# A reordered attention loop: fewer TensorE mode switches per head pair, q/k turned two pairs ahead, both heads normalised at once, V staging buffers of their own

## The chip, the cores and the metric

The kernel runs on one core of a Trainium2 chip. The metric is device time in microseconds (us) of one execution; a profile adds the "span", from the first to the last instruction, which is about 1.7 us shorter than the time. A single core has no second, slower die to be compared with, so the state of a run is judged by its time: one that is more than 1.5% above the fastest run of the same kernel is marked slow. Each kernel has one profile, of its first run (that of before is of a run apart); three that I use fell in runs marked slow (before, and the experiments e3 and f1).

## The reference, cut to what matters

Causal attention with 16 extra "beacon" keys and values in front, for 8 batches of 8 heads (576 tokens, 64 wide), then a soft mixture of experts over the 4608 tokens of width 512: 8 experts with 4 slots each.

```python
k_all = concat([beacon_k, k]); v_all = concat([beacon_v, v])
a = softmax(q @ k_all.T / 8, causal over the 576 own keys)
x = (a @ v_all) as 4608 x 512
logits = x @ phi                                # 4608 x 32
d = softmax(logits, over tokens);  slot_input = d.T @ x
for e in range(8):
    slot_out[e] = relu(slot_input[e] @ w1[e]) @ w2[e]
out = softmax(logits, over slots) @ slot_out
```

## The kernel before

The loop works on 32 pairs of heads. For one pair it makes scores in four "score steps" (K x Q products into PSUM, then an exp on ACT; step 0 also gets a causal mask on POOL), multiplies by V with a column of ones ("attend", which gives the sums too), divides by the sums on DVE, and turns the result ("xt_piece") for the logits. q and k of a later pair are transposed on TensorE in a 64-row mode ("transp"); the score steps are 64-row work too, nearly everything else is 128-row work (dt is 32-row). Once per batch of four pairs there are three more pieces: logits, the turned weights d ("dt"), and the sums for the slots ("si"). All of the expert weights are read during the loop into one large tile, the arena. Then come the expert stage and the output stage.

`vbuf[1]`, the landing place of V for odd batches, is a piece of the arena, and so are the q/k slots:

```python
arena = const.tile([P, E * 8192], F16, name="arena")
# load_pair: q and k of pair n go to arena[:, o:o + ...]         (five slots)
vmore = const.tile([P, TK * D], F16, name="vmore")
vbuf = [vmore[:, :], arena[:, vend:vend + TK * D]]
...
def load_bv(b):                       # beacon V: every fourth partition
    nc.gpsimd.dma_start(out=vbuf[b % 2][0:4 * H:4, 0:Nb * D], in_=beacon_v[b]...)
```

The order of one pair (cut):

```python
score(n, 0);  xt_piece(n - 2);  score(n, 1)
transp(n + 1)
attend(n - 1, 0)                      # reciprocal and product of head 0
score(n, 2)
attend(n - 1, 1)                      # reciprocal and product of head 1
score(n, 3)
load_pair(n + 5)
```

`avs` are two tiles of one PSUM bank each, `scs` two tiles of two banks each:

```python
avs = [ps_av.tile([P, 512], FP, name=f"av{i}") for i in range(2)]
scs = [ps_sc.tile([P, 2, 512], FP, name=f"sc{i}") for i in range(2)]
...
sop = avs[0]                                        # sum of the second layers
def first_layer(e):
    hp = avs[1] if e % 2 else scs[0][:, 0, :]       # hidden layer of expert e
    ...16 matmuls into hp, then Relu on ACT: hp -> hbuf
for e in range(E + 2):
    first_layer(e)       # if e < E
    turn_hidden(e - 1)   # 2 transposes, 1 copy
    second_layer(e - 2)  # 8 matmuls into sop
```

The softmax here doesn't subtract the row's maximum and nothing guards it: scores larger than these inputs give would overflow.

## Time and profile before

| | before |
|---|---|
| time of the runs, us | 227.32 median (225.67 to 228.94) |
| span of the profile, us | 231.3 (this run, of 233.0 us, is marked slow) |
| first mask of pair 0 to that of pair 5 | 35.1 |
| first mask of pair 5 to that of pair 31 | 132.0 |
| slot sums ready to expert outputs ready ("expert stage") | 16.5 |

The first mask of a pair is a good milestone, because POOL does exactly one such mask per pair, after the first exp. It is not exact: when POOL is held by its DMA issues, the mask comes later than the exp's end (in before by 1.1 to 3.3 us in pairs 0, 1, 2, 8 and 24).

The page's head, busy time per engine and the slices of the TensorE clock and of DMA (one digit is 1/40 of the span, 9 is 90% or more):

```profile
span 231.3 us, 7829 instructions
...
PE 169.4 (73%) x3400; PEld 119.7 (52%) x3400; DVE 145.8 (63%) x365; ACT 135.4 (59%) x187; POOL 88.6 (38%) x151
...
PEclk9999999999979999956999999799999967999965
DMA  6999299998599999969899994998699990029996
```

No engine is full. The DMA row dips to 2, 5, 6 and 4 in slices 5, 11, 18 and 25 (of 5.8 us each), in a stretch where there is always something left to load: something holds loads back there.

The list of waits (engine, line, what it waited for: us in total, times, longest), first TensorE's, its weight loads (PEld) and its matmuls (PE):

```profile
PEld L240 <- DMA arena<-in_beacon_v_dram: 9.6, 4, 3.2
PE tr L240 <- DMA arena<-in_beacon_v_dram: 8.3, 4, 3.0
```

And the waits of the queue on SP that issues q and k loads:

```profile
SPq L90 <- DMA arena<-in_beacon_v_dram: 40.5, 4, 10.5
```

Line 240 is the q/k transposes, line 90 the q/k loads. Neither has any business with beacon V. The timeline around the second of the four occurrences (start, duration, engine, line, operation, in brackets the idle time before and what ended it):

```profile
61.70 0.53 POOL L143 DMA_DIRECT2D arena<-in_beacon_v_dram  x1 [3.45 <-DMA arena<-in_k_dram]
...
63.55 0.78 PE L240 MATMUL tr<-idb,arena 64*64 64x64 bf16 x36 [3.00 <-DMA arena<-in_beacon_v_dram]
63.56 0.33 SPq L90 DMA_DIRECT2D arena<-in_q_dram  x1
```

POOL sits 3.45 us until all k loads in flight have landed, then issues one small load; TensorE and the q/k queue are released together when it has landed. It is a fence in both directions, and it occurs four times, once per odd batch. Even batches use the same strided load into another tile and have no such wait.

Stretches of the windows view (length, busy time of each engine with its number of instructions, granted clock, DMA share, GB/s landed):

```profile
core 0: us, PE busy (x) PEld busy (x) DVE busy (x) ACT busy (x) POOL busy (x), PEclk, DMA share, GB/s
58.00:64.00 6.00, 2.56 (x66) 1.79 (x66) 2.99 (x8) 3.26 (x4) 2.54 (x5) 1.00 0.49 86
64.00:100.00 36.00, 31.40 (x713) 23.63 (x708) 28.43 (x70) 24.74 (x36) 19.33 (x33) 0.93 1.05 263
188.00:204.40 16.40, 13.66 (x244) 7.01 (x245) 3.66 (x11) 10.33 (x8) 0.00 (x0) 0.82 0.16 33
...
196.00:200.00 4.00, 3.72 (x91) 2.41 (x92) 1.09 (x5) 2.54 (x3) 0.00 (x0) 1.00 0.01 4
```

Inside a fence the DMA share is 0.49; outside it is about 1. The third row is the expert stage: 16.4 us and clock 0.82. It starts at 0.50 and, as the last row shows, is at 1.00 in its second half.

Away from fences a pair takes about 4.6 us. TensorE has no long wait there, but each score step and each transposition waits a little for DVE or ACT:

```profile
131.50 0.40 PE L255 MATMUL sc<-qT,kT 64*128 64x128 bf16 x8 [0.24 <-ACT ex L261]
132.12 0.43 PE L304 MATMUL tr<-idh,xb 128*128 128x128 f16 x5 [0.22 <-DVE xb L290]
```

### The profile page before, as it was taken

The numbers are of one execution on the slowest core, as the hardware profiler recorded it, in microseconds if no ns is written. First come the engines' busy times: TensorE is split into PE (matmuls) and PEld (weight loads), VectorE is DVE, ScalarE is ACT, GpSimd is POOL, SyncE is SP. The second block draws the span as 40 slices with busy tenths as digits, with TensorE's granted clock in tenths as the row PEclk, the third lists the DMA queues.
The fourth block names the chain that finished last, engine by engine and source line by source line (L and its number), as shares of the span: only waits on it lengthen the run. The fifth ranks groups of instructions, "written<-read, shape, count | busy, mean of one in ns | idle before, by whom it ended". The sixth has DMA issues, their size and how long they took to land.

```text
span 231.3 us, 7829 instructions
## 1 busy us (share of the span) xinstructions
PE 169.4 (73%) x3400; PEld 119.7 (52%) x3400; DVE 145.8 (63%) x365; ACT 135.4 (59%) x187; POOL 88.6 (38%) x151
## 2 busy tenths in 40 slices
PE   2624469888498998799988986988898759878300
PEld 1413257666285766577666664756766535433100
DVE  4409267868566997875689777568966622279500
ACT  2531416796548678744966877395797338659400
POOL 8380435454448545433647435253464300000000
PEclk9999999999979999956999999799999967999965
DMA  6999299998599999969899994998699990029996
GB/s 203 247 312 243 27 240 263 207 258 203 91 225 280 244 283 288 257 131 207 246 205 262 265 270 114 201 316 152 106 198 213 214 192 7 3 99 422 415 424 272
DMA packets 20049, 50.89 MB, mean 220 GB/s; under 512 B 5169, under 2 KB 5169, under 8 KB 18992
## 3 DMA queue, kind: packets, MB, share of 16 engines
q0 software_dynamic: 7776, 21.77, 50.0%
q1 hardware_dynamic: 12096, 28.35, 34.0%
q8 instruction: 26, 0.43, 0.7%
q10 hardware_dynamic: 144, 0.29, 0.3%
q14 instruction: 7, 0.06, 0.1%
HBM read 62.71 MB, written 9.44 MB: 312 GB/s over the span
## 4 chain that ended last, share of the span: by engine, by line
PE 32%; DMA 26%; DVE 22%; ACT 8%; issue 3%; SPq 1%; POOL 1%; DVEq 0%; POOLq 0%; ACTq 0%
PE av L282 9%; DMA arena<-in_k_dram 7%; PE tr L240 6%; DMA phif<-in_moe_phi_dram 6%; PE sc L255 6%; DVE xb L290 5%; DVE arena L515 4%; DMA arena<-in_q_dram 4%; ACT ex L261 4%; DMA arena<-in_beacon_v_dram 3%; DMA vmore<-in_v_dram 3%; DVE qT L242 3%; DVE vh L133 3%; PE tr L304 3%; DVE kT L242 3%
## 5 line engine op out<-in xcount | busy, mean ns | idle before, releaser
L261 ACT ACTIVATE ex<-sc 128x1024 f16<-128x1024 f32 (+3 forms) x128 | 106.0, 868 | 66.5 <-PE sc L255 66.3
L263 POOL TENSOR_SCALAR_AFFINE_SELECT ex<-ex 128x1024 f16<-128x1024 f16 x32 | 35.1, 1095 | 65.7 <-ACT ex L261 65.7
L255 PE MATMUL sc<-qT,kT 64*128 64x128 bf16 (+5 forms) x576 | 48.9, 267 | 6.8 <-ACT ex L261 5.4
L282 PEld LDWEIGHTS <-ex 128*128 128x128 f16 (+2 forms) x960 | 40.8, 114 | 11.2 <-issue 10.0
L282 PE MATMUL av<-vh,ex 128*128 128x65 f16 (+1 forms) x896 | 45.0, 207 | 2.1 <-DVE vh L133 2.1
L240 PE MATMUL tr<-idb,arena 64*64 64x64 bf16 x1152 | 29.7, 204 | 20.8 <-DMA arena<-in_beacon_v_dram 8.3
L242 DVE COPY qT<-tr 128x576 bf16<-128x576 bf16 x32 | 24.2, 757 | 27.4 <-PE tr L240 27.4
L240 PEld LDWEIGHTS <-arena 64*64 64x64 bf16 x1152 | 25.4, 118 | 28.9 <-issue 11.7
L290 DVE TENSOR_TENSOR xb<-av,r 128x320 f16<-128x320 f32 x64 | 31.5, 492 | 2.2
L255 PEld LDWEIGHTS <-kT 64*128 64x128 bf16 (+1 forms) x576 | 21.2, 105 | 18.3 <-issue 11.9
L242 DVE COPY kT<-tr 128x576 bf16<-128x576 bf16 x32 | 24.0, 750 | 1.7 <-PE tr L240 1.5
L308 DVE COPY xT<-tr 128x592 f16<-128x592 f16 x32 | 14.4, 449 | 8.6 <-PE tr L304 8.6
L304 PE MATMUL tr<-idh,xb 128*128 128x128 f16 (+1 forms) x160 | 14.7, 226 | 4.6 <-DVE xb L290 4.4
L161 POOL DMA_DIRECT2D arena<-in_moe_w_dram x32 | 17.8, 556 | 0.0
L289 DVE RECIPROCAL r<-av 128x5 f32<-128x5 f32 x64 | 12.1, 190 | 5.2 <-PE av L282 4.7
L304 PEld LDWEIGHTS <-xb 128*128 128x128 f16 (+1 forms) x160 | 9.6, 101 | 9.8 <-DVE xb L290 8.5
L282 PE MATMUL av<-vt,ex 80*80 80x65 f16 x64 | 13.6, 213 | 0.9 <-DVE vt L133 0.9
L133 DVE STREAM_TRANSPOSE vh<-vmore 128x512 f32<-128x512 f32 x8 | 8.8, 1122 | 7.2 <-DMA arena<-in_v_dram 7.2
L513 ACT ACTIVATE arena<-fp,rc 128x512 f32<-128x512 f32 x18 | 11.3, 686 | 3.4 <-PE fp L511 2.7
L515 DVE TENSOR_SCALAR arena<-fp,rc 128x512 f32<-128x512 f32 x18 | 12.3, 746 | 0.7 <-PE fp L511 0.7
L511 PE MATMUL fp<-soh,eLh 128*128 128x512 f16 x36 | 10.6, 377 | 2.4 <-ACT arena L513 1.5
L269 POOL TENSOR_SCALAR_AFFINE_SELECT ex<-ex 80x160 f16<-80x160 f16 x32 | 10.3, 323 | 2.6 <-ACT ex L261 2.3
(66 smaller groups left out, 143.0 us busy)
## 6 DMA issues: line engine op xcount, KB each, us to landing
arena<-in_moe_w_dram POOLq DMA_DIRECT2D x32, 512.0 KB, 8.7
arena<-in_q_dram SPq DMA_DIRECT2D x32, 288.0 KB, 7.1
arena<-in_k_dram SPq DMA_DIRECT2D x31, 288.0 KB, 8.7
out_dram<-arena SPq DMA_DIRECT2D x8, 1024.0 KB, 8.6
arena<-in_v_dram POOLq DMA_DIRECT2D x20, 128.0 KB, 6.5
vmore<-in_v_dram POOLq DMA_DIRECT2D x15, 128.0 KB, 6.8
out_dram<-arena SPq DMA_DIRECT2D x2, 512.0 KB, 3.0
arena<-in_k_dram ACTq DMA_DIRECT2D x1, 288.0 KB, 2.7
```

Of the source, the lines that this page charges most:

```text
L133: nc.vector.transpose(out=dst[:, e], in_=src.bitcast(FP).rearrange("p (j e) -> p e j", j=TK)[:, e])
L161: nc.gpsimd.dma_start(out=arena[:, wloc[m]:wloc[m] + WP], in_=src)
L240: nc.tensor.transpose(tp[po:po + 64, j, :], hi, idb[po:po + 64, po:po + 64])
L242: nc.vector.tensor_copy(out=dst[:, Nb:Nb + S].rearrange("p (s j) -> p s j", j=J), in_=tp[:, :, :].rearrange("p j s -> p s j"))
L255: nc.tensor.matmul(sc[0:kn, a, col:col + un], kT[n % 3][64 * a:64 * a + 64, P * c:P * c + kn], qT[n % 3][64 * a:64 * a + 64, u0:u0 + un], ...
L261: nc.scalar.activation(ex[n][:, :, o:o + w], sc[:, :, 0:w], AF.Exp, scale=scale)
L263: nc.gpsimd.affine_select(out=ex[n][:, :, 0:512].rearrange("p a (c t) -> p a c t", c=4), in_=ex[n][:, :, 0:512].rearrange("p a (c t) -> p ...
L282: nc.tensor.matmul(avs[a][0:m, i * DD:(i + 1) * DD], ex[n][0:kn, a, o:o + m], vchunk(b, h, c, kn), start=(c == 0), stop=(c == i))
L290: nc.vector.tensor_tensor(out=xb[b % 2][:, :, h, :], in0=avv[:, :, 0:D], in1=r5[:, :].unsqueeze(2).broadcast_to([P, NCH, D]), op=AL.mult)
L304: nc.tensor.transpose(tp[:, i, 0:m], xb[b % 2][0:m, i, 2 * g:2 * g + 2, :].rearrange("p h d -> p (h d)"), idh[0:m, 0:m])
L308: nc.vector.tensor_copy(out=xT[b][:, g, :], in_=tp[:, :, :].rearrange("p i u -> p (i u)")[:, 0:U])
L515: nc.vector.tensor_scalar(out=osb[:, j, :], in0=fp_[:, :], scalar1=rc[:, i:i + 1], scalar2=None, op0=AL.mult)
```

## The change

The intent: switch TensorE between 64-row and 128-row work twice per pair instead of six times, by putting score steps 3, 0 and 1 and the q/k transposes next to each other; turn q and k two pairs ahead instead of one; normalise both heads with one reciprocal and one product; give both V buffers tiles of their own; land the first V batch so that beacons need no strided load. The diff, cut to its core:

```diff
-    vmore = const.tile([P, TK * D], F16, name="vmore")
-    vbuf = [vmore[:, :], arena[:, vend:vend + TK * D]]
-    vlast = arena[:, vend + TK * D:vend + 2 * TK * D]
+    vbuf = [const.tile([P, TK * D], F16, name=f"vbuf{i}") for i in range(2)]
+    vlast = arena[:, vend:vend + TK * D]
+    vto = vend + TK * D
...
-    vt = [const.tile([P, 4 * H, DP], F16, name=f"vt{i}") for i in range(2)]
+    vt = [arena[:, vto:vto + 4 * H * DP].rearrange("p (r d) -> p r d", d=DP),
+          const.tile([P, 4 * H, DP], F16, name="vt1")]
...   # first V batch: partitions in order (chunk, head); its beacons in partitions 0..7
-    wloc = [...] + [lend + WP * x for x in (3, 4, 5, 6, 7, 0, 1, 2)]
+    wloc = [...] + [lend + WP * x for x in (6, 7, 3, 4, 5, 0, 1, 2)]
...
-    avs = [ps_av.tile([P, 512], FP, name=f"av{i}") for i in range(2)]
+    av = ps_av.tile([P, 2, 512], FP, name="av")
...   # transp: beacon columns of kT copied by POOL first, not by DVE last
...   # attend: both heads, then
+        r5 = sml.tile([P, 2, NCH], FP, name="r5", tag="r5")
+        nc.vector.reciprocal(out=r5[:, :, :], in_=avv[:, :, :, D])
+        nc.vector.tensor_tensor(out=xb[b % 2][:, :, 2 * g:2 * g + 2, :]..., in0=avv[:, :, :, 0:D], ...)
...   # the loop
+        score(n, 0)
+        score(n, 1)
+        xt_piece(n - 2)
+        attend(n - 1)
+        score(n, 2)
+        transp(n + 2)
+        load_pair(n + 7)
+        score(n, 3)
+        # then, once per batch each: logits (two halves), dt_piece, si_piece
...   # the expert stage
-    sop = avs[0]
+    sop = av[:, 0, :]
-        hp = avs[1] if e % 2 else scs[0][:, 0, :]
+        hp = av[:, 1, :] if e % 2 else scs[0][:, 0, :]
```

More of the change, by code (lines that the diff above doesn't have):

```diff
@@ L106, in load_v @@
     def load_v(b, qd):
-        main = vbuf[b % 2]
-        lo = (32 * qd - Nb) * D
-        if b == 0 and qd == 0:
-            nc.gpsimd.dma_start(out=main[0:1, Nb * D:TK * D], in_=vrows[0:1, 0:(TK - Nb) * D])
+        lo = b * H * S * D + (32 * qd - Nb) * D
+        hs_, cs_ = [S * D, H], [4 * TK * D, 4]
+        if b > 0:
             nc.gpsimd.dma_start(
-                out=main[1:4, :],
-                in_=bass.AP(tensor=v.tensor, offset=v.offset + lo + 4 * TK * D,
-                            ap=[[4 * TK * D, 3], [1, TK * D]]))
-            nc.gpsimd.dma_start(
-                out=main[4:32, :],
-                in_=bass.AP(tensor=v.tensor, offset=v.offset + S * D + lo,
-                            ap=[[S * D, H - 1], [4 * TK * D, 4], [1, TK * D]]))
-            return
@@ L120, in load_v @@
-        nc.gpsimd.dma_start(
-            out=main[32 * qd:32 * qd + 32, :],
-            in_=bass.AP(tensor=v.tensor, offset=v.offset + b * H * S * D + lo,
-                        ap=[[S * D, H], [4 * TK * D, 4], [1, TK * D]]))
+                out=vbuf[b % 2][32 * qd:32 * qd + 32, :],
+                in_=bass.AP(tensor=v.tensor, offset=v.offset + lo, ap=[hs_, cs_, [1, TK * D]]))
+        elif qd > 0:
+            nc.gpsimd.dma_start(
+                out=vbuf[0][32 * qd:32 * qd + 32, :],
+                in_=bass.AP(tensor=v.tensor, offset=v.offset + lo, ap=[cs_, hs_, [1, TK * D]]))
+        else:
+            nc.gpsimd.dma_start(out=vbuf[0][0:H, 0:Nb * D],
+                                in_=beacon_v[0].rearrange("h n d -> h (n d)"))
+            nc.gpsimd.dma_start(out=vbuf[0][0:H, Nb * D:TK * D], in_=vrows[0:H, 0:(TK - Nb) * D])
+            nc.gpsimd.dma_start(
+                out=vbuf[0][H:32, :],
+                in_=bass.AP(tensor=v.tensor, offset=v.offset + lo + 4 * TK * D,
+                            ap=[[4 * TK * D, 3], hs_, [1, TK * D]]))
@@ L136, in turn_v @@
     def turn_v(b, hf):
-        turn(vh[b % 2].bitcast(FP).rearrange("p c h e -> p e h c"), vbuf[b % 2], hf)
+        turn(vh[b % 2].bitcast(FP).rearrange("p c h e -> p e c h" if b == 0 else
+                                             "p c h e -> p e h c"), vbuf[b % 2], hf)
     def turn_tail(b4, hf):
@@ L152 @@
     WP = 2048
-    wloc = [m * WP for m in range(24)] + [lend + WP * x for x in (3, 4, 5, 6, 7, 0, 1, 2)]
+    wloc = [m * WP for m in range(24)] + [lend + WP * x for x in (6, 7, 3, 4, 5, 0, 1, 2)]
     def load_w(m):
@@ L189 @@
         load_tail(0, i)
-    load_bv(0)
     idh = const.tile([P, P], F16, name="idh")
@@ L210 @@
     bkT = const.tile([P, NP, Nb], BF, name="bkT")
-    avs = [ps_av.tile([P, 512], FP, name=f"av{i}") for i in range(2)]
-    for a_ in avs:
-        nc.vector.memset(a_[64:P, 4 * DD:5 * DD], 1.0)
+    av = ps_av.tile([P, 2, 512], FP, name="av")
+    nc.vector.memset(av[64:P, :, 4 * DD:5 * DD], 1.0)
     scs = [ps_sc.tile([P, 2, 512], FP, name=f"sc{i}") for i in range(2)]
@@ L233, in transp @@
     def transp(n):
+        nc.gpsimd.tensor_copy(out=kT[n % 3][:, 0:Nb], in_=bkT[:, n, :])
         for (f, dst) in ((qf, qT[n % 3]), (kf, kT[n % 3])):
@@ L241, in transp @@
                                         idb[po:po + 64, po:po + 64])
-            nc.vector.tensor_copy(
-                out=dst[:, Nb:Nb + S].rearrange("p (s j) -> p s j", j=J),
-                in_=tp[:, :, :].rearrange("p j s -> p s j"))
-        nc.vector.tensor_copy(out=kT[n % 3][:, 0:Nb], in_=bkT[:, n, :])
+            nc.vector.tensor_copy(out=dst[:, Nb:Nb + S].rearrange("p (s j) -> p s j", j=J),
+                                  in_=tp[:, :, :].rearrange("p j s -> p s j"))
     ex = {}
@@ L272, in score, with attend @@
                 pattern=[[0, 2], [1, UL]], channel_multiplier=-1)
-    def attend(n, a):
+    def attend(n):
         b, g = divmod(n, H // 2)
-        h = 2 * g + a
-        for i in range(NCH):
-            m = P if i < 4 else UL
-            for c in range(i + 1):
-                kn = P if c < 4 else UL
-                o = blk[(c, i)]
-                nc.tensor.matmul(
-                    avs[a][0:m, i * DD:(i + 1) * DD],
-                    ex[n][0:kn, a, o:o + m],
-                    vchunk(b, h, c, kn),
-                    start=(c == 0), stop=(c == i))
-        r5 = sml.tile([P, NCH], FP, name="r5", tag="r5")
-        avv = avs[a][:, 0:NCH * DD].rearrange("p (i d) -> p i d", d=DD)
-        nc.vector.reciprocal(out=r5[:, :], in_=avv[:, :, D])
+        for a in range(2):
+            for i in range(NCH):
+                m = P if i < 4 else UL
+                for c in range(i + 1):
+                    kn = P if c < 4 else UL
+                    o = blk[(c, i)]
+                    nc.tensor.matmul(
+                        av[0:m, a, i * DD:(i + 1) * DD],
+                        ex[n][0:kn, a, o:o + m],
+                        vchunk(b, 2 * g + a, c, kn),
+                        start=(c == 0), stop=(c == i))
+        r5 = sml.tile([P, 2, NCH], FP, name="r5", tag="r5")
+        avv = av[:, :, 0:NCH * DD].rearrange("p a (i d) -> p a i d", d=DD)
+        nc.vector.reciprocal(out=r5[:, :, :], in_=avv[:, :, :, D])
         nc.vector.tensor_tensor(
-            out=xb[b % 2][:, :, h, :], in0=avv[:, :, 0:D],
-            in1=r5[:, :].unsqueeze(2).broadcast_to([P, NCH, D]), op=AL.mult)
+            out=xb[b % 2][:, :, 2 * g:2 * g + 2, :].rearrange("p i a d -> p a i d"),
+            in0=avv[:, :, :, 0:D],
+            in1=r5[:, :, :].unsqueeze(3).broadcast_to([P, 2, NCH, D]), op=AL.mult)
     xT = {}
@@ L348 @@
     wl = 0
-    for n in range(NP + 1):
+    for n in range(NP):
         b, g = divmod(n, H // 2)
-        last = n == NP
-        if not last:
-            score(n, 0)
-            if n >= 2:
-                xt_piece(n - 2)
-            if n >= 6 and g == 2:
-                logit_piece(b - 1, 0)
-            if n >= 6 and g == 3:
-                dt_piece(b - 1)
-            score(n, 1)
-            if n >= 6 and g == 2:
-                logit_piece(b - 1, 1)
-        if n + 1 < NP:
-            transp(n + 1)
+        score(n, 0)
+        score(n, 1)
         if n == 0:
+            transp(1)
+            load_pair(5)
+            load_pair(6)
             nc.vector.tensor_copy(out=idh[:, :], in_=idb[:, :])
@@ L370 @@
                 turn_tail(0, hf)
+        if n >= 2:
+            xt_piece(n - 2)
+        if n >= 1:
+            attend(n - 1)
+        score(n, 2)
+        if n + 2 < NP:
+            transp(n + 2)
+            if n + 7 < NP:
+                load_pair(n + 7)
+        score(n, 3)
+        if n >= 5 and g == 1:
+            logit_piece(b - 1, 0)
+        if n >= 6 and g == 2:
+            logit_piece(b - 1, 1)
+        if n >= 6 and g == 3:
+            dt_piece(b - 1)
+        if n >= 8 and g == 0:
+            si_piece(b - 2)
@@ L371 @@
         if n == 1:
+            beacons(1, B)
             nc.vector.tensor_copy(out=phih[:, :, :, :],
                                   in_=phif[:, :, :].unsqueeze(2).broadcast_to([P, NDC, 4, NSL]))
+        if n == 1:
+            for qd in range(4):
+                load_v(1, qd)
         if n == 2:
-            beacons(1, B)
-        if last:
-            xt_piece(n - 2)
-        if n >= 1:
-            attend(n - 1, 0)
-        if not last:
-            score(n, 2)
-        if n >= 1:
-            attend(n - 1, 1)
@@ L384 @@
-        if n >= 8 and g == 0 and not last:
-            si_piece(b - 2)
-        if not last:
-            score(n, 3)
-        if last:
-            si_piece(B - 2)
-            xt_piece(n - 1)
-            logit_piece(B - 1, 0)
-            logit_piece(B - 1, 1)
-            dt_piece(B - 1)
-            si_piece(B - 1)
-        if not last:
-            if n + 5 < NP:
-                load_pair(n + 5)
-            if b + 1 < B and g in (2, 3):
-                turn_v(b + 1, g - 2)
-            if n == 0:
-                for qd in range(4):
-                    load_v(1, qd)
-            if n == 1:
-                load_bv(1)
-            if n in (2, 3):
-                load_v(2, 2 * n - 4)
-                load_v(2, 2 * n - 3)
-                if n == 3:
-                    load_bv(2)
-            if n >= 4 and b + 2 < B:
-                load_v(b + 2, g)
-                if g == 3:
-                    load_bv(b + 2)
-            if 8 <= n < 11:
-                load_tail(1, n - 8)
-            if 13 <= n < 15:
-                turn_tail(1, n - 13)
-            want = 23 * (n + 1) // 28 if n < 28 else (25, 28, 30, 32)[n - 28]
-            while wl < want:
-                load_w(wl)
-                wl += 1
@@ new lines @@
+            load_bv(1)
+        if n == 3:
+            turn_v(1, 0)
+            turn_v(1, 1)
+        if 1 <= b < B - 1 and g in (2, 3):
+            turn_v(b + 1, g - 2)
+        if n == 3:
+            for qd in range(4):
+                load_v(2, qd)
+        if n >= 4 and b + 2 < B:
+            load_v(b + 2, g)
+            if g == 0 and b == 1:
+                load_bv(2)
+            if g == 3:
+                load_bv(b + 2)
+        if 8 <= n < 11:
+            load_tail(1, n - 8)
+        if 13 <= n < 15:
+            turn_tail(1, n - 13)
@@ L424 @@
+        want = 24 * (n + 1) // 28 if n < 28 else (26, 28, 30, 32)[n - 28]
+        while wl < want:
+            load_w(wl)
+            wl += 1
+    xt_piece(NP - 2)
+    attend(NP - 1)
+    si_piece(B - 2)
+    xt_piece(NP - 1)
+    logit_piece(B - 1, 0)
+    logit_piece(B - 1, 1)
+    dt_piece(B - 1)
+    si_piece(B - 1)
     dsum = const.tile([P, 1], FP, name="dsum")
```

## The prediction

> **What bounds the kernel now.** The timeline splits the 231.3 us span into start (0 to 46), pair loop (to 183), expert layers (to 205) and output. The change touches the first two. No engine is full: the page gives PE 73%, DVE 63%, ACT 59%, POOL 38%.
>
> 1. Undisturbed pairs. On the ACT timeline the exps of step 0 start at 113.5, 119.3, 123.8 and, two pairs on, 132.0: some 4.6 us a pair. Busy per pair: ACT 3.4 plus 0.3 for logits; DVE about 4.2 (q and k copies 0.76+0.75, beacon columns 0.16, two reciprocals and products 2 x 0.68, xT 0.45, V turns about 0.6). The ring is serial: k transposes, copies, both normalisations, then at once the xT transposes that PE waits for (PE tr L304 behind DVE xb, 4.4 us), score step 1, next transposes. PE changes between 64-row and 128-row work six times a pair.
>
> 2. Four stalls, not of compute. The list of waits has SP waiting 40.5 us, PE's q/k transposes 8.3 and their weight loads 9.6, for "arena<-in_beacon_v_dram", four times each: the beacon-V loads of odd batches (POOL timeline: 26.6, 61.7, 103.0, 143.3). That strided destination lies in the arena beside the q/k slots, so I read it as a false dependency: POOL waits for the q/k loads, then q/k transposes and new loads wait for it. The windows show DMA share 0.25, 0.49, 0.52, 0.45 around them, against 0.94 to 1.05 elsewhere; around the third the granted clock is 0.5. I put their cost at 13 to 20 us: the first 4 to 8, the others 3 to 5 each.
>
> **What changes.** Both V buffers leave the arena, so the beacon load should no longer fence q/k: the largest item. Four of six mode switches go; the Trainium skill (TensorEngine Tiling (Array Packing), Key Properties) says a mode change drains TensorE. The trace agrees in kind: weight loads wait 0.17 to 0.40 us for "issue" there; I estimate 0.1 to 0.2 us of true PE time per switch. DVE loses 0.16 (beacon columns, to POOL) and about 0.35 a pair (one 640-element product, estimated 0.83, for 2 x 0.49; one reciprocal for two): 4.2 to about 3.65. The xT transposes get two score steps of slack. The new ring (exp of step 2, scores 0 and 1, xT, both heads, score 2) I estimate at 4.05 us, 4.2 to 4.3 with logits and V turns.
>
> **Limit.** Per pair the loads read about 1.7 MB of HBM (0.59 q/k, 0.26 V, 0.86 weights, f32). From 64 to 100 us the measured 263 GB/s of landed bytes is about 400 GB/s read (the casts halve bytes), share 1.05: about 4.25 us a pair. DMA becomes the next bound; weights may lag until the experts.
>
> **Sum.** First exp of pair 5 at about 38 instead of 45.7; 26 pairs x 4.3 = 112 instead of 132; rest unchanged, 53.6. Span about 204 against 231; scaled to the unprofiled 227.3, about 201. With some DMA shortage, 205.
>
> **Right if:** no wait for beacon-V loads on SP or PE; no low DMA slice between 20 and 60 us or in mid-loop; pairs near 4.3 us; xT transposes wait hardly at all; 32 products at about 0.83 us; loop ends near 155 to 160.
>
> **Wrong if:** the V tail tile moved into the arena makes new false waits; POOL, now owner of beacon columns, holds up scores behind its DMA issues; DMA saturates well below 400 GB/s, or late weights stall the experts; batching two heads lengthens the ring.
>
> Faster by over 2%: 93%; within 2%: 6%; slower: 1%. Predicted 205 us, 80% range 197 to 216.

## The result, and the profile after

| | before | after |
|---|---|---|
| time, us, median of 4 runs of the same rounds | 228.13 (225.67 to 231.01, the last one slow by the rule above) | 216.51 (215.91 to 216.55) |
| ratio after/before, 95% interval | | 0.952 (0.943 to 0.961): faster |
| span of the profile, us | 231.3 | 214.2 |
| first mask, pair 0 to pair 5 | 35.1 | 29.2 |
| first mask, pair 5 to pair 31 | 132.0 | 116.5 |
| expert stage | 16.5 | 22.5 |

A ratio is the mean time of one kernel's fast runs over that of the other's fast runs of the same rounds, so not quite the ratio of the medians quoted. The change is 4.8% faster. The prediction was 205 us with a range of 197 to 216; the measured time is 216.5, so half of the expected gain is missing.

The page of after:

```profile
span 214.2 us, 7748 instructions
...
PE 155.8 (73%) x3400; PEld 113.4 (53%) x3400; DVE 135.3 (63%) x268; ACT 133.6 (62%) x187; POOL 92.0 (43%) x182
...
PEclk9999699799999999999999999999997555899955
DMA  6999999999999999999999999977999300059996
```

The DMA dips of the loop are gone, as predicted. But the clock has a new stretch of 7, 5, 5, 5, 8 at slices 31 to 35, where before has a 6 and a 7 at slices 33 and 34: that is the expert stage. No transpose and no q/k load waits for beacon V any more. These lines are new (L316 and L328 are logits and dt, L483 the experts' second layer, L242 the q/k transposes; "issue" means that the profile shows nothing that was waited for):

```profile
PE tr L316 <- DVE qT L244: 8.4, 13, 0.7
...
PE tr L328 <- DVE qT L244: 3.8, 6, 0.9
...
PE av L483 <- ACT hbuf L470: 3.3, 3, 1.1
...
PE tr L242 <- issue: 3.3, 5, 1.1
```

The windows of after:

```profile
58.00:100.00 42.00, 33.84 (x877) 26.86 (x877) 32.45 (x61) 31.33 (x47) 24.73 (x49) 1.00 1.06 266
165.00:188.00 23.00, 17.96 (x246) 8.82 (x247) 3.73 (x12) 10.44 (x8) 0.00 (x0) 0.59 0.13 25
...
175.80:181.20 5.40, 4.27 (x60) 2.09 (x57) 0.86 (x3) 1.51 (x2) 0.00 (x0) 0.50 0.01 3
```

The loop now keeps DMA full where before had a fence, at the same rate as outside of fences. The expert stage does the same number of matmuls as before (246 against 244, by the window's edges), with the clock at 0.59 instead of 0.82, so the same matmuls are busy for 18.0 us instead of 13.7. In the second half of the stage, where before is at 1.00, after is still at 0.50. A piece of that stage:

```profile
171.24 1.30 ACT L470 ACTIVATE hbuf<-av 128x256 f16<-128x256 f32 x1 [0.82 <-PE av L465]
...
172.59 1.04 PE L483 MATMUL av<-arena,hbuf 128*32 128x512 f16 x8 [1.08 <-ACT hbuf L470]
```

TensorE goes through first layer of expert e, turning of e - 1, second layer of e - 2. The second layer of expert 1 has had its input since the turn before, and yet it starts only when the Relu of expert 3 has ended, at 171.24 + 1.30 = 172.54. The same happens behind the Relus of experts 5 and 7. In before no second layer waits for a Relu.

And a pair of the loop, for the ring that the prediction had put at 4.05 us, or 4.2 to 4.3 with pieces:

```profile
97.15 0.65 PE L316 MATMUL tr<-xT,phih 128*128 128x288 f16 x4 [0.65 <-DVE qT L244]
...
100.00 0.82 DVE L290 TENSOR_TENSOR xb<-av,r 128x640 f16<-128x640 f32 x1
100.74 0.75 DVE L244 COPY qT<-tr 128x576 bf16<-128x576 bf16 x1
...
101.54 0.65 PE L316 MATMUL tr<-xT,phih 128*128 128x288 f16 x4 [0.65 <-DVE qT L244]
```

One pair to the next is 101.54 - 97.15 = 4.39 us. The q/k transposes were done early enough, but their copy on DVE queues behind the product of both heads, and the logit matmuls need the PSUM buffer which that copy frees. So the ring runs through the one large product.

### The profile page after: what moved, and what is told of

The parts are those of the page before. It is cut to its first block, busy times and chain, and to the rows that moved or that the text cites. A ratio compares the mean times of both kernels' runs of the same rounds, so it can differ in the third digit from the quotient of the medians.

```text
span 214.2 us, 7748 instructions
## 1 busy us (share of the span) xinstructions
PE 155.8 (73%) x3400; PEld 113.4 (53%) x3400; DVE 135.3 (63%) x268; ACT 133.6 (62%) x187; POOL 92.0 (43%) x182
## 4 chain that ended last, share of the span: by engine, by line
PE 39%; DVE 32%; DMA 9%; ACT 6%; issue 6%; SPq 1%; POOL 1%; DVEq 0%; ACTq 0%
PE av L282 12%; DVE xb L290 9%; DVE qT L244 7%; PE sc L255 7%; DMA arena<-in_k_dram 5%; DVE arena L513 5%; PE tr L305 4%; PE tr L316 4%; DMA arena<-in_moe_w_dram 4%; PE av L483 3%; ACT ex L261 3%; DVE vh L135 3%; DVE r L289 3%; ACT hbuf L470 2%; DVE kT L244 2%
## 5 line engine op out<-in xcount | busy, mean ns | idle before, releaser
L255 PE MATMUL sc<-qT,kT 64*128 64x128 bf16 (+5 forms) x576 | 42.7, 254 | 4.7 <-POOL kT L235 3.0
L282 PE MATMUL av<-vh,ex 128*128 128x65 f16 (+1 forms) x896 | 38.6, 200 | 1.2 <-issue 1.2
L282 PEld LDWEIGHTS <-ex 128*128 128x128 f16 (+2 forms) x960 | 37.0, 110 | 1.9 <-issue 1.6
L242 PE MATMUL tr<-idb,arena 64*64 64x64 bf16 x1152 | 26.9, 198 | 7.7 <-DMA arena<-in_q_dram 3.7
L242 PEld LDWEIGHTS <-arena 64*64 64x64 bf16 x1152 | 22.6, 113 | 15.5 <-issue 9.1
L290 DVE TENSOR_TENSOR xb<-av,r 128x640 f16<-128x640 f32 x32 | 26.4, 824 | 1.1
L244 DVE COPY qT<-tr 128x576 bf16<-128x576 bf16 x32 | 23.9, 747 | 4.6 <-PE tr L242 4.5
L244 DVE COPY kT<-tr 128x576 bf16<-128x576 bf16 x32 | 23.9, 747 | 1.0 <-PE tr L242 1.0
L135 DVE STREAM_TRANSPOSE vh<-vbuf 128x512 f32<-128x512 f32 x16 | 17.8, 1128 | 1.5 <-DMA arena<-in_v_dram 1.5
L289 DVE RECIPROCAL r<-av 128x10 f32<-128x10 f32 x32 | 7.1, 220 | 16.3 <-PE av L282 16.3
L316 PE MATMUL tr<-xT,phih 128*128 128x288 f16 x64 | 10.4, 284 | 8.6 <-DVE qT L244 8.4
L111 POOL DMA_DIRECT2D vbuf<-in_v_dram x28 | 15.7, 567 | 0.0
L320 ACT ACTIVATE eLh<-tr 128x288 f16<-128x288 f32 x16 | 6.6, 412 | 13.6 <-PE tr L316 13.6
L477 DVE COPY hbuf<-tr 128x256 f16<-128x256 f16 x8 | 2.3, 292 | 17.1 <-PE tr L476 17.1
## 6 DMA issues: line engine op xcount, KB each, us to landing
arena<-in_k_dram SPq DMA_DIRECT2D x31, 288.0 KB, 11.2
```

The source lines that it names most:

```text
L111: nc.gpsimd.dma_start(out=vbuf[b % 2][32 * qd:32 * qd + 32, :], in_=bass.AP(tensor=v.tensor, offset=v.offset + lo, ap=[hs_, cs_, [1, TK * ...
L135: nc.vector.transpose(out=dst[:, e], in_=src.bitcast(FP).rearrange("p (j e) -> p e j", j=TK)[:, e])
L242: nc.tensor.transpose(tp[po:po + 64, j, :], hi, idb[po:po + 64, po:po + 64])
L244: nc.vector.tensor_copy(out=dst[:, Nb:Nb + S].rearrange("p (s j) -> p s j", j=J), in_=tp[:, :, :].rearrange("p j s -> p s j"))
L255: nc.tensor.matmul(sc[0:kn, a, col:col + un], kT[n % 3][64 * a:64 * a + 64, P * c:P * c + kn], qT[n % 3][64 * a:64 * a + 64, u0:u0 + un], ...
L282: nc.tensor.matmul(av[0:m, a, i * DD:(i + 1) * DD], ex[n][0:kn, a, o:o + m], vchunk(b, 2 * g + a, c, kn), start=(c == 0), stop=(c == i))
```

## The experiments

Thirteen kernels ran, on four chips; each timed in three rounds beside before. A difference between kernels of two calls is less sure than one within a call, since the chip is another. The labels' letters stand for the call (e, f, g, h). "Correct" and "wrong result" speak of the kernel's output, not of the expectation. "Undisturbed pair" is the difference of first masks that repeats most in the loop.

The theories after seeing the result: the fence was worth all that the measured gain shows (A) or the new order was worth it (B); the batching of two heads lengthens the ring (R); the loop is bound by the DMA engines, or by stops of TensorE's instruction supply under that load (I); the expert stage lost time to a dependency made by sharing a PSUM tile (X), or to the clock as such (C).

### e1: before, with the V buffers out of the arena and nothing else

```diff
-    vbuf = [vmore[:, :], arena[:, vend:vend + TK * D]]
+    vbuf = [const.tile([P, TK * D], F16, name=f"vbuf{i}") for i in range(2)]
     (with vlast, vt[0] and the order of wloc as in after)
```

> Before, with one thing of the change: both V buffers leave the arena (the first tail tile takes the place). Theory A, the false fence of the four beacon-V loads was the main cost before: 211 to 218 us, no wait for beacon-V loads, no DMA slice under 0.6 in the loop. Rival B, the new TensorE order made the gain: 223 to 228 us. If the expert stage runs at half clock, as in the trace of after, some 6 us more than A says.

Correct; 218.82 us, ratio 0.952 (0.945 to 0.958). No wait for beacon V on TensorE or SP. The median is 0.8 us above theory A's range, in a call where before took 230.2. Pair 0 to 5 fell from 35.1 to 30.7 us, pair 5 to 31 from 132.0 to 122.7: together 13.7 us, but before's profile is of a slow run; by the fast runs' times the move is worth 4.8% of 230 us, about 11 us. The move of the buffers alone gives the whole gain of the change. The beacon loads kept their stride and only left the arena. In before, unstrided loads into the arena (V, weights) hold up neither the q/k transposes nor the q/k queue, so stride and sharing seem to be needed both; no run tested the stride. So the reordering either gave nothing, or gave something that was lost elsewhere.

### e2: after, with the odd V buffer back in the arena

```diff
-    vbuf = [const.tile([P, TK * D], F16, name=f"vbuf{i}") for i in range(2)]
+    vbuf = [vmore[:, :], arena[:, vend:vend + TK * D]]
     (with vlast, vt and wloc as in before)
```

> After, with one thing undone: the second V buffer is in the arena again. Theory A: three or four fences return, 226 to 232 us, waits for beacon-V loads of 20 us or more on SP. Rival B: under 220 us. With q/k turned two pairs ahead the fences may cost less than in before, then 220 to 226.

Correct; 238.8 us, ratio 1.039 (1.030 to 1.048): slower than before. Four pairs take 9.3 to 11.2 us instead of 4.39. TensorE's wait:

```profile
PE tr L241 <- DMA arena<-in_beacon_v_dram: 23.9, 4, 8.0
```

The same four fences cost TensorE 23.9 us here against the 8.3 of before. This was more than either theory expected. With q/k turned and loaded further ahead, each fence has more loads in flight to wait for: that is a reading of the longer waits, not a separate test. What is shown: without the move of the buffers, the rest of the change would have been a loss.

### e3: after, with the heads normalised one by one, in two PSUM tiles

```diff
-    av = ps_av.tile([P, 2, 512], FP, name="av")
+    avs = [ps_av.tile([P, 512], FP, name=f"av{i}") for i in range(2)]
     # in attend, a reciprocal and a product after each head, as in before
-    sop = av[:, 0, :]
+    sop = avs[0]
-        hp = av[:, 1, :] if e % 2 else scs[0][:, 0, :]
+        hp = avs[1] if e % 2 else scs[0][:, 0, :]
```

> After, with one thing undone: each head has its own reciprocal and product, issued right after its matmuls. Theory R, the pair is bound by the ring attend, normalise, qT copy, logit piece (waits for its PSUM buffer 0.65 us), scores: head 0 is normalised under the matmuls of head 1, qT copy starts about 0.3 us earlier, undisturbed pairs go from 4.38 to about 4.1 us, total 208 to 213. Rival D, vector time counts: 0.34 us more of it a pair, 219 to 226. Rival M, DMA holds the pairs: same within 1 us.

Correct; 210.1 us, ratio 0.911 (0.902 to 0.919): the fastest correct kernel, and faster than both given ones. Two things changed at once. The undisturbed pair fell from 4.39 to 4.16 us, and the expert stage from 22.5 to 17.25 us. But pair 5 to 31 took 118.4 us, no less than after's 116.5 (this profile fell in a run marked slow). So the shorter ring is real, and yet it did not shorten this loop; the total fell within theory R's range by the expert stage, not by the ring. What filled it is seen in TensorE's timeline: stops for which the profile shows no releaser.

```profile
73.23 0.62 PE L339 MATMUL tr<-dT,xb 128*128 128x32 f16 x18 [0.64 <-issue]
...
91.62 0.22 PE L243 MATMUL tr<-idb,arena 64*64 64x64 bf16 x2 [1.28 <-issue]
```

The second is in the middle of a run of 36 transposes that have everything they need. Counting the instructions from the start of the span to each stop (windows view):

```profile
0.00:73.21 73.21, 53.96 (x1245) 42.70 (x1245) 55.24 (x130) 45.44 (x61) 45.25 (x92) 0.98 1.01 258
...
0.00:91.60 91.60, 68.67 (x1628) 54.38 (x1629) 71.00 (x165) 58.78 (x80) 55.50 (x112) 0.98 1.02 261
```

Matmuls and weight loads add up to 2490 and 3257, and 3257 - 2490 = 767 is three times 256, less one. All ten stops of more than 0.3 us in the loop of e3 come at a count of 182 to 188 modulo 256 (the count drifts down slowly, as it would if some records are missing); they sum to 7.6 us. The six such stops of after come at 184 to 188 as well, and those of f1, f2, f3 and f4 in the same place. Three later kernels have the very loop of e3: h1, g1 and g4 show 6, 13 and 11 such stops from pair 5 on, 6.1 to 8.9 us.

### e4: after, with half of the expert weights not loaded

```diff
+    for m in range(1, 32, 2):
+        wloc[m] = wloc[m - 1]
     def load_w(m):
+        if m % 2:
+            return
```

> After, wrong result on purpose: every second weight piece is not loaded, its place shared with the one before, so 16.8 of 62.7 MB are not read. Theory R: undisturbed pairs stay at 4.38 us, only the pairs that wait for q/k shorten, total 211 to 215. Rival M, DMA is the bound: pairs at 4.1 us or less, total under 208.

Wrong result; 211.85 us, ratio 0.912 (0.902 to 0.922). DMA share in the loop fell from 1.03 to 0.81, the undisturbed pair stayed at 4.39, pair 5 to 31 took 117.9 us. With the ring of after, the load on DMA is not what sets the pairs. Most of the gain lies in the expert stage, 17.9 us, where the clock was 0.90; its three waits (0.88, 1.25 and 0.89 us) are still there. That the stage's clock rose in this kernel is not explained.

### f1: after, with one line of the expert stage changed

```diff
-    sop = av[:, 0, :]
+    sop = scs[1][:, 0, :]
```

> After, one line changed: the sum of the expert layers goes to a score tile, so that it no longer shares a PSUM tile with the odd experts' hidden rows. Theory X, making one tile of the two head accumulators fences the experts: the three waits of 1.1 us of second-layer matmuls behind the odd Relus go, the TensorE clock of the stage rises, the stage (siz to soh) takes 17 to 18 us instead of 22.5, ratio to before 0.92 to 0.935. Rival, the half clock there is chance or comes from elsewhere: stage 21 to 22.5 us, ratio 0.945 to 0.955.

Correct; 211.79 us, ratio 0.919 (0.900 to 0.939). The wait is gone, the stage takes 17.1 us at clock 0.76. In the same place as shown for after, the second layer now runs while the Relu does:

```profile
174.52 1.33 ACT L470 ACTIVATE hbuf<-av 128x256 f16<-128x256 f32 x1 [0.82 <-PE av L465]
...
174.72 1.04 PE L483 MATMUL sc<-arena,hbuf 128*32 128x512 f16 x8
```

The built instruction list says the same before anything runs (it is no run; it comes out of building the two kernels): in after three second-layer matmuls carry a wait for ACT, in f1 none does. In both kernels the sum and the hidden layer lie in different PSUM banks; what differs is whether the two banks belong to one tile. The wait is thus made by the tile, not needed by the chip: the Trainium skill (PSUM — Partial Sum Buffer, "PSUM bank collisions raise a hardware error") says that two engines on different banks run clean, and f1's correct results agree.

This also gives the worth of the reordering, across calls. f1 has both changes and no expert wait: from e1's 0.952 to f1's 0.919 is 3.2% of 228, about 7 us; and from after's 0.952 to f1's 0.919 is again about 7 us, which the sharing of the tile had taken back. The interval of f1 is wide, from two fast runs; the traces give 5.4 us for the stage, and 6.3 us between e1 and f1, about half of them before pair 5.

### h1: e3, with the shared tile put back into the expert stage

```diff
-    sop = avs[0]
+    sop = scs[1][:, 0, :]
-        hp = avs[1] if e % 2 else scs[0][:, 0, :]
+        hp = scs[1][:, 1, :] if e % 2 else scs[0][:, 0, :]
```

> Heads apart (e3), and only the tile sharing of the expert stage put back: the second-layer sum and the hidden rows of the odd experts are the two halves of one score tile. Theory X: the three waits of about 1.1 us behind the Relus of experts 3, 5 and 7 return, the stage takes 18 us (clock near 0.9) to 22.5 us (clock near 0.6) instead of 17.2, ratio 0.915 to 0.935 against e3's 0.911. Rival, the long stage of after came from the work before it: no such waits, stage 16.2 to 17.3 us.

Correct; 215.28 us, ratio 0.942 (0.935 to 0.950), against e3's 0.911: even more than expected. The stage is back at 22.5 us with clock 0.62, and the waits are back, in a tile that has nothing to do with the heads:

```profile
PE sc L483 <- ACT hbuf L470: 3.5, 3, 1.2
```

All kernels, ordered by whether sum and odd hidden layers share a tile ("expert stage" is slot sums ready to outputs ready):

| kernel | shared tile | stage, us | granted clock |
|---|---|---|---|
| before, e1 | no | 16.5, 17.2 | 0.82, 0.75 |
| e3, f1, f2, f3, f4, g2, g3 | no | 16.5 to 17.25 | 0.75 to 0.81 |
| g1, g4 (filler matmuls) | no | 16.2, 16.2 | 1.00, 1.00 |
| after, e2, h1 | yes | 22.5, 21.2, 22.5 | 0.59, 0.69, 0.62 |
| e4 (half the weights) | yes | 17.9 | 0.90 |

The three waits add up to 3.3 us, the stage loses 5 to 6. The low clock must have a part in it: e4 has the waits at a clock of 0.90, and its stage is only about 1 us longer than those without. On the clock, the Trainium skill (TensorE: Matmul & The Clock Gate, Part 1) says that the array is throttled to half by default and falls back to it after an idle window. The profile agrees in kind: in before the stage starts at 0.50 and climbs to 1.00, in after it is still at 0.50 after 16 us, though no long idle stretch is seen there (TensorE is busy for 79 to 87% of it). That the waits bring it about is the reading that fits after, e2 and h1, but e4 has the waits and a clock of 0.90, so the clock does not follow from them every time. That sharing the tile lengthens the stage is shown; how the waits and the clock divide the loss is not.

### f2 and f4: pieces of the batch moved ahead of score step 2

f2 is f1, f4 is e3, each with logits, dt and si pieces issued right after the attend, where no q copy is in the way:

```diff
         attend(n - 1)
+        (logit_piece, dt_piece, si_piece as below)
         score(n, 2)
         transp(n + 2); load_pair(n + 7)
         score(n, 3)
-        (logit_piece, dt_piece, si_piece)
```

> f1, and the logit, dT and slot-sum pieces are issued right after the heads, before score step 2, so that their PSUM buffer is free. Theory R, the pair is bound by the ring through the normalisation and the qT copy: waits of these pieces for qT (14 us in after) go, undisturbed pairs fall from 4.39 to 3.9 to 4.1 us, ratio 0.89 to 0.91. Rival M, DMA or instruction supply: undisturbed pairs shorten, but others lengthen, the mean from pair 5 to 31 stays at 4.4 to 4.5, ratio as f1. If ACT's logit exp ahead of step 2 lengthens the ring: pairs 4.4.

> Heads apart (e3) and pieces early: the shortest ring I know. Theory M, the loop is near its DMA limit at about 4.25 to 4.5 us a pair with the full data: ratio 0.895 to 0.91, no better than e3 (0.911) by more than 1.5%. Theory R alone: pairs at 3.9 us, ratio under 0.88.

Both correct. The local effect came: in f2 the waits of these pieces for the q copy vanish, and pairs with the second half of the logits take 4.12 us instead of 4.39. The total did not: f2 214.4 us, ratio 0.938 (0.930 to 0.947), against f1's 0.919; f4 216.37 us, ratio 0.936 (0.921 to 0.951), against e3's 0.911. Pair 5 to 31 took 119.3 and 120.7 us. Pairs with the other pieces stay at 4.3 to 4.4, and in f2 7.8 us of waits for exps from pair 5 to 31 (0.2 in f1) took the place of those for the q copy. Neither expectation's ratio was met. f2's interval overlaps f1's, and their pairs 5 to 31 take the same 119.3 us, so that f2 is slower than f1 is not shown; f4's interval lies above e3's, which ran in another call, and why was not found.

### f3 and g2: e3 with half, and with one thirty-second, of the weights

f3 has e4's edit on e3. g2 loads a single piece:

```diff
+    wloc = [0] * 32
     def load_w(m):
+        if m:
+            return
```

> Heads apart (e3) with half of the weight pieces, wrong on purpose. In e3 undisturbed pairs took 4.16 us but the mean was 4.55. Theory M, loads hold the other pairs: mean 4.2 to 4.3, pair 5 to 31 in 108 to 112 us, ratio 0.87 to 0.885, DMA share below 0.95. Rival, the lengthening has nothing to do with the amount of data: mean stays at 4.5, ratio about 0.91.

> Heads apart (e3), wrong on purpose: only one of 32 weight pieces is loaded, 32.5 of 62.7 MB are not read. Theory I, PE's stops at every 256th instruction (counts 0.72 modulo 256 in all traces) are late refills of its instructions behind data: no stop over 0.38 us from pair 5 on, nearly all pairs at 4.17, pair 5 to 31 in 108 to 111 us (118.4 in e3, 114.8 with half the weights). Rival, the stops do not depend on data traffic: three or more stay, 113 us or more.

Wrong results. All with the ring of e3:

| kernel | DMA share, pairs 5 to 31 | stops over 0.3 us | undisturbed pair | mean pair | ratio |
|---|---|---|---|---|---|
| e3, all weights | 1.04 | 10 | 4.16 | 4.55 | 0.911 (0.902 to 0.919) |
| f3, half | 0.83 | 3 | 4.17 | 4.41 | 0.900 (0.890 to 0.910) |
| g2, 1/32 | 0.55 | 0 | 4.16 | 4.20 | 0.873 (0.867 to 0.880) |

With the loads gone, the stops are gone and the mean pair sits on the ring. Half the weights gave only a part, less than f3 expected. The stops of e3, 7.6 us, are three quarters of the (4.55 - 4.16) x 26 = 10.1 us between its mean and its undisturbed pairs (two thirds, if the pairs are taken from exp to exp). So e3's shorter ring is eaten by a loaded DMA, mostly through stops at every 256th TensorE instruction. (g2 also spares POOL 31 load issues of 0.56 us; the part outside the stops could come from there.) The refills themselves stand in the trace, as a DMA queue of kind "instruction" (packets, MB, share of the engines); e3's page:

```profile
q8 instruction: 26, 0.43, 0.8%
```

Each of the 26 packets has 16384 bytes, and the 6800 matmuls and weight loads of TensorE are 26.6 blocks of 256. In the packed trace every one of e3's ten stops ends 1.3 to 1.6 us after such a packet has landed, and all 76 stops over 0.3 us from pair 5 on, over all kernels, do so within 1.2 to 1.7 us. So the stops are late refills. From pair 5 on the packet starts, in the median, about 3.7 us after TensorE has passed the last boundary in e3, 2.7 in f3 and 1.1 in g2: the load delays it. One limit of this: before and e1 ran at shares of 0.92 and 0.99 without one such stop. Their packets start about 2.6 and 2.4 us after the boundary, early enough; why they start earlier than e3's at nearly the same share is open.

### g1: e3 with filler matmuls that keep the clock up

Two 512-column matmuls into an unused bank after each first layer, and nine around the last pieces.

```diff
             first_layer(e)
+            warm(2)
```

> Heads apart (e3) with dummy matmuls of 512 columns where PE waits in the expert stage and just before it; their results are never read. Theory C, the half clock of the first third of the stage costs time: TensorE clock of the stage 0.9 or more, siz to soh 14 to 15.5 us instead of 17.2, ratio 0.895 to 0.905. Rival, the Relus on ACT (1.3 us each) bound the stage: 16.5 to 17.5 us, ratio as e3 (0.911) within 0.7%.

Correct; 213.48 us, ratio 0.928 (0.919 to 0.937): no gain, and outside the ranges of both theories. The clock in the stage was 1.00 instead of 0.75, but the stage took 16.2 us instead of 17.25. The stage's chain of work that ended last, from 167 to 184 us, runs through TensorE: 14 of the 16 fillers are on it, with 3.8 us, and of the eight Relus only the last. So this way of keeping the clock up does not pay, but what a full clock would be worth without fillers is not tested. The output stage took 28.1 us instead of 26.7 (in g4 too), for a reason that stays open.

### g3: f1 with the first V batch landed the old way

```diff
     # load_v(0, .) head-major as in before, and
+    load_bv(0)
```

> f1 with one more thing undone: the first V batch is laid out as in before (head-major, beacon rows written over afterwards). If the chunk-major layout matters: V batch 0 is turned 2 to 4 us later (13.4 us in after, 17.5 in before) and the first mask of pair 5 comes 1 to 3 us later than the 40.1 us of f1, ratio 0.925 to 0.935. Rival, the start is bound by q/k of pair 2 or by the bandwidth of the start: pair 5 within 0.7 us, ratio as f1 within 0.7%.

Correct; 212.86 us, ratio 0.926 (0.916 to 0.935), against f1's 0.919 (0.900 to 0.939). V is turned at 15.65 us instead of 14.39; pair 5's mask comes 1.2 us later, its exp only 0.2. So the chunk-major landing is worth at most about 1 us; the times do not resolve it.

### g4: g1 with pair 0's beacon columns copied by DVE

```diff
-        nc.gpsimd.tensor_copy(out=kT[n % 3][:, 0:Nb], in_=bkT[:, n, :])
+        (nc.gpsimd if n else nc.vector).tensor_copy(out=kT[n % 3][:, 0:Nb], in_=bkT[:, n, :])
```

> g1 and the beacon columns of the first pair copied by DVE, not by POOL behind its DMA issues and a memset (PE waited 3.0 us for it in after). If that wait is on the path of the start: first score near 6.8 us instead of 8.7, pair 5 about 1 us earlier, ratio 0.5% under g1. Rival, V batch 0 and q/k of pair 2 set the start: no difference.

Correct; 213.19 us, ratio 0.926 (0.916 to 0.936), the same as g1. In after the very first score waits 3.0 us for POOL's copy, which queues behind POOL's first loads; with DVE it starts earlier (6.77 us) and pair 5's mask comes at 38.7 instead of 41.1, but the time does not show it.

## Why the prediction was wrong, and where it was right

**The sum, term by term**, in us of span, against after's trace:

| term of the prediction | predicted | after | missed by |
|---|---|---|---|
| first exp of pair 5 | 38 | 37.4 | -0.6 |
| 26 pairs to the first exp of pair 31 | 112 (4.3 each) | 117.6 (4.52 each) | 5.6 |
| "rest unchanged, 53.6" | 53.6 | 59.2 | 5.6 |
| span | 203.6, given as "about 204" | 214.2 | 10.6 |

Two terms fail, by the same amount; for one of them the experiments settle the cause.

**The step that failed is "rest unchanged, 53.6".** The rest did change: against its 5.6 us too many, the expert stage alone has 6.0 more, 22.5 us instead of 16.5. I read the diff's `sop = av[:, 0, :]` and `hp = av[:, 1, :]` as renaming. They put the sum and the odd hidden layers into one tile, so three second layers wait for a Relu, and in these traces TensorE goes on at a low clock. f1 undoes that line alone and gets 0.919, which times 228.1 is 209.7 us, inside the predicted range; h1 puts it back into e3 and loses it again. Two kernels, two different tiles, one effect: this cause is shown.

**The second term off is "26 pairs x 4.3".** The undisturbed pair is 4.39, and the mean, from exp to exp, 4.52. The prediction listed "batching two heads lengthens the ring" among what would make it wrong, yet its sum booked the batching as a saving of 0.35 us of DVE time. DVE time was not on the ring; the delay of the q copy behind the 0.82 us product is. Of the kernels in after's order, every one with the heads apart has an undisturbed pair of 4.16 and every one with them together 4.38 or 4.39. In the time it is hardly seen: h1, which is after with the heads apart and a like sharing of a tile, has 0.942 (0.935 to 0.950) against after's 0.952 (0.943 to 0.961). The ring explains 2.3 of the 5.6 us. The rest is not settled: after has five stops of 4.2 us in these pairs, but with half the weights (e4) the pairs were no shorter; and pair 5 alone took 6.06 us, at a granted clock of 0.76. In e3 the excess over its ring is the loaded DMA, which the prediction expected in kind ("DMA becomes the next bound", 4.25 us a pair) but as a bandwidth; what g2 and e3 show is largely stops of TensorE between instructions.

**Right**: the fence, in its mechanism. Its cost was put at 13 to 20 us; e1 against before gives 13.7 in the traces, of which before's is slow, and by the fast runs' times (0.952) about 11, so the range was high. No beacon-V wait is left on TensorE or SP, the DMA dips are gone, the product of both heads took 0.824 us each of 32 times (0.83 estimated), the last product of the loop starts at 159.5 (loop end "near 155 to 160"), and the xT transposes wait for a product twice, 0.9 us in all, where before had 4.4. The "wrong if" item of false waits by the new tenant of the arena did not come about. Late weights cost nothing: the first expert matmul is put down to a wait of 1.0 us for one, but it starts 0.06 us after the slot sums. POOL's copy of beacon columns held up one score, the first, by 3.0 us.

**Not decided**: the share of the mode switches. The reordering as a whole is worth about 7 us (e1 against f1), and the ring, the lead of q/k and the switches change in it together. The Trainium skill (TensorEngine Tiling (Array Packing), Key Properties) states that a mode change drains TensorE; where weight loads wait for "issue" at a switch, it is 0.17 to 0.40 us in before and 0.17 to 0.24 in after's loop. But other switches show only 0.03 to 0.15 us, and in before 0.40 us also stands between loads of one mode, so the prediction's "the trace agrees in kind" is too strong; no run took the switches alone. Four of six switches did not go either: with the batch pieces a pair has 4 left, of 6 to 8.

**What remains open**: what else lengthens after's pairs; why f4 is slower than e3; why the output stage is 1.4 us longer in g1; why e4's stage kept a high clock with the waits; why the refills of before and e1 start earlier.

**The best version** of what ran is e3 (0.911): the change's order and buffers, the old normalisation head by head. f1 (0.919) overlaps with it.

## What to carry to other kernels

When a diff moves a tile, follow it to every later stage that borrows it: two PSUM banks made into one tile tie their readers and writers together, and a small strided load into a shared tile can fence the other users of that tile. Here the first cost about 7 us and the second about 11, against about 7 that the reordering gains, and both can be read ahead, one as a wait that names data the waiting instruction does not use, the other in the built list of instructions. A prediction's "the rest is unchanged" is a claim like any other, so check the lines of the diff that fall into the rest.

## What the Trainium skill lacked or had wrong

- Runtime: NRT & Kernel Launch, "Instruction fetch mechanics": it says that instructions are refilled in blocks of 256 and that crossing a boundary is "mostly hidden". The 256 agrees with where TensorE stops here. Hidden it was not: in the loop of e3, at a DMA share of 1.04, ten stops of 0.33 to 1.57 us add up to 7.6 us, in f3 one took 1.91; at a share of 0.55 (g2) none exceeds 0.3. A word on busy DMA queues would help. Each stop of e3 ends 1.3 to 1.6 us after an "instruction" packet of 16384 bytes has landed.
- No page that I found tells of dependencies by tile. PSUM — Partial Sum Buffer speaks of banks, and is right about them (f1 is correct with the two engines in two banks at once); but two banks of one tile gave three waits of about 1.1 us and a stage of 22.5 instead of 17.1 us. Likewise a strided load into a tile shared with other buffers gave four fences, about 11 us in before by the times of e1 and 23.9 us of TensorE waits in e2.
- TensorE: Matmul & The Clock Gate, Part 1: agrees in kind, and tells of short idles without a measure for judging a stage with short waits: clock 0.59 with three waits of 1.1 us (after), 0.90 with three of 0.9 to 1.25 us (e4), 0.76 with none (f1). TensorE busy for 79 to 87% of the first 16 us of after's stage stayed at 0.50; in before the clock climbed in 4 us in which it was busy for 94%.
- TensorEngine Tiling (Array Packing), Key Properties: no cost is given for the drain at a mode switch. The traces here do not give it: weight loads wait 0.17 to 0.40 us at some switches and 0.03 to 0.15 at others.
